# Second network's out stage by one level of Strassen's algorithm, in two passes per group of 768 tokens

## The chip, the cores and the metric

One core of a Trainium2 chip runs the whole program. The metric is the time of one execution on the device in microseconds (us); the median of three executions is quoted. TensorE does the matrix products (PE in the rows; PEld is its loading of weights), VectorE (DVE), ScalarE (ACT) and GpSimd (POOL) do the elementwise work, SyncE (SP) issues the transfers between the chip's DRAM, where all arrays lie, and the on-chip buffers.

## The reference, cut to what matters

```python
x = attention(q, k, v, f)            # 2304 tokens x 512, causal, with decay; unchanged here
h = x @ w_in                         # 512 x 2048, first network
x = (h / (1 + exp(-h))) @ w_out      # 2048 x 512, "first out stage"
a = x @ w_a                          # 512 x 1536, second network
b = x @ w_b
return (a * b) @ w_out2              # 1536 x 512, "second out stage"
```

Everything is computed from float32 to float32. Each float32 product is done as three matrix products of rounded halves: an operand is split into a high part and the rest (low part), and high times high, high times low and low times high are added up in PSUM.

## The kernel before

**Stages.** After the attention (to about 190 us) come four stages, each of which keeps TensorE full: the first network's in stage, its out stage, the second network's in stage, its out stage. Tokens are handled in 3 groups of 768 (`GT`, two halves of 384 = `HB`).

**In stages.** They already use one level of Strassen's algorithm. The input of a group is cut into 2 x 2 blocks, seven sums of blocks (`FORMS`) are formed and split by `make_forms` into the buffers `X0`, `X1`, `X2`, the weights of a unit by `load_unit` into `wA`, `wB`, `wC`. A `job` (one unit, one group) does seven products (`product`, L709) of 6 matmuls of 128 x 384 and combines them on ACT and DVE (L751 to L792). In the second network it also multiplies a by b and sends the result to the array `cdram` by `send` (L740).

**Out stages.** `out_blocks` takes blocks of 512 tokens (four of them, and one of 256): for each of the 16 (first) or 12 (second) pieces of 128 rows it loads the piece from DRAM into one of seven slots (`ring`, L819), splits it (ACT cast L823, DVE subtraction L824, tile `hl`, tag `u` of three slots) and does 12 matmuls (L832) into four PSUM banks. At a block's end ACT and DVE copy the banks and SP sends them out (L858 to L860). There is no Strassen step here.

**Weights.** They arrive as float64 bits and are decoded by `decode`, piece by piece (128 x 512): a transfer of 512 KB (`raw`, L656), one ACT operation (L658), four DVE operations (L659, L660, L662, L663) and one POOL addition (L664). `load_out` decodes the 12 pieces of the second out stage around its start, and splits them with ACT (L612) and POOL (L613) into the tiles `wo`, which lie in `X2` and `X0` once the in stage's inputs there are used up.

**What sets the order.** All operations are put into a `Plan`, with a duration, a priority and what they read and write; `Plan.order` sorts them by a list schedule, in which every engine takes the operation that can start first. The engines then run the result in that fixed order, each waiting where its next instruction's data or buffer isn't ready. `split` does a cast on ACT and a subtraction on the engine given (`pool` or `ss`, that is POOL or DVE).

Of the kernel before, what the change touches and what calls it, by code (L numbers as in the profile page):

```python
# [18 lines left out]
P = 128  # L19
# [212 lines left out]
def model_kernel(ctx: ExitStack, tc: tile.TileContext, qk, q0, v, f, w, out):  # L232
# [21 lines left out]
    rows_sb = dp.tile([NH, 6, 2, S], BF16, name="rows")  # L254
    gdram = dram.tile([F1, P, NT], F32, name="gdram")
    cdram = dram.tile([F2, P, NT], F32, name="cdram")
# [458 lines left out]
    def bank(tag, name):  # L715
        return buf(mm if tag == "mm" else aps, tag, [P, 512], F32, name)

    def job(stage, u, g, t, early):
# [54 lines left out]
        if stage == 0:  # L773
            gate(1, 1, d, at(4) - 2)
        else:
            z = zbuf()
            dve(HB, lambda e: e.tensor_mul(z()[:, 1], pc(1), pd()), [(c, 1), d], [(z, 0, 1)], at(4) - 2)
# [11 lines left out]
        if stage == 0:  # L789
            gate(1, 0, a, at(6) - 2)  # L790
        else:
            dve(HB, lambda e: e.tensor_mul(z()[:, 0], pc(0), pa()), [a, (c, 0)], [(z, 0, 0)], at(6) - 2)  # L792
            send(0, rows(cdram, u), at(6))

    def load_out(stage, h, slot, pr):
        nf = (F1, F2)[stage] // 2
# [6 lines left out]
        yield  # L803

# [49 lines left out]
    def evict_end(t0, n, ps, p):  # L854
        for oc in range(KC):
            o = buf(zp, "z", [P, n], F32, f"out_{t0}_{oc}")
            reads, writes = [ps[oc]], [o]
            plan.add("ACT", 190 + n / 1.2, lambda o=o, oc=oc: nc.scalar.copy(o(), ps[oc]()[:, :n]), reads, writes, p,  # L858
                     also=[("DVE", 160 + n / 0.96, lambda o=o, oc=oc: nc.vector.tensor_copy(o(), ps[oc]()[:, :n]))])
            plan.dma(480, 4 * P * n, lambda o=o, oc=oc: nc.sync.dma_start(out[oc * P:(oc + 1) * P, t0:t0 + n], o()), [o], [("out", t0, oc)], p)  # L860
# [95 lines left out]
    for n, blocks in enumerate(SETS):  # L956
# [75 lines left out]
```

## Time and profile before

| | |
|---|---|
| median of 3 runs | 969.08 us (968.35 to 969.65) |
| profiled execution | 969.41 us, span 967.5 us |
| granted TensorE clock | 1.0 of full speed |
| first out stage | 353.6 to about 551 us |
| second in stage | about 551 to 816.1 us |
| second out stage | 816.1 to 964.1 us, then 3.4 us to the end |

The span is the time from the first instruction to the last; what the execution has beyond it, 1.9 us, lies around the program. Operations of an engine that is not waited for cost nothing, so each number below counts only where TensorE would wait for it, or at the end of the program.

### The profile page before, as it was taken

To read this page: it belongs to the slowest core of one execution; us is meant where nothing else is said; L and a number is where in the kernel's file an instruction comes from. 1 tells how busy PE (TensorE), PEld (TensorE's weight loads), DVE (VectorE), ACT (ScalarE), POOL (GpSimd) and SP (SyncE) were. 2 spreads that over 40 slices of the span, in tenths; PEclk is the share of its full clock that TensorE was granted. 3 is DMA by queue.
4 is the path that set the end of the run, shared out by engine and by line. 5 is a ranking of instruction groups with operands and counts; after the bars stand their busy time and mean duration, and the time that the engine had idled before them with its cause. 6 is when DMAs were issued, how large, how long until landed. Compare 5 with 4: busy or idle time off the path is not lost.

```text
span 967.5 us, 16086 instructions
## 1 busy us (share of the span) xinstructions
PE 959.0 (99%) x5760; PEld 854.4 (88%) x5760; DVE 649.0 (67%) x1284; ACT 483.6 (50%) x1067; POOL 383.7 (40%) x350
## 2 busy tenths in 40 slices
PE   8999999999999999999999999999999999999998
PEld 7766666899999998888888999999999999888888
DVE  7878898985777889778622685765655684932222
ACT  5898888955566664347332543433333332423222
POOL 5677886102585435455100034754444450510000
PEclk9999999999999999999999999999999999999999
DMA  5544433222455586354431103423233336446422
GB/s 154 178 164 146 152 118 114 86 107 106 159 202 185 171 304 221 103 181 142 142 98 49 39 34 110 137 93 109 93 116 109 115 93 228 163 112 184 134 67 93
DMA packets 56560, 128.41 MB, mean 133 GB/s; under 512 B 9500, under 2 KB 14764, under 8 KB 56448
## 3 DMA queue, kind: packets, MB, share of 16 engines
q1 hardware_dynamic: 56368, 126.94, 40.2%
q8 instruction: 45, 0.74, 0.3%
q10 hardware_dynamic: 112, 0.45, 0.2%
q14 instruction: 35, 0.29, 0.1%
HBM read 89.08 MB, written 38.26 MB: 132 GB/s over the span
## 4 chain that ended last, share of the span: by engine, by line
PE 90%; DVE 5%; DMA 1%; ACT 1%; issue 1%; SPq 1%; POOL 0%; DVEq 0%; ACTq 0%
PE o L832 34%; PE a L709 25%; PE b L709 12%; PE g L709 6%; PE s L450 4%; PE pv L572 3%; PE t_x L526 2%; PE t_y L526 2%; DMA rb<-invs 1%; DVE x L613 1%; DVE z L626 1%; DVE p L476 1%; PE idle L297 1%; PE s L444 1%; SPq L505 1%
## 5 line engine op out<-in xcount | busy, mean ns | idle before, releaser
L832 PE MATMUL o<-hl,wo 128*128 128x512 f32 (+1 forms) x1680 | 346.4, 368 | 0.1
L832 PEld LDWEIGHTS o<-hl,wo 128*128 128x128 f32 x1680 | 292.6, 189 | 53.5 <-DVE hl L824 1.3
L709 PE MATMUL a<-x,w 128*128 128x384 f32 x1440 | 270.4, 334 | 0.1
L709 PEld LDWEIGHTS a<-x,w 128*128 128x128 f32 x1440 | 251.2, 188 | 0.8 <-DVE d L772 0.5
L824 DVE TENSOR_TENSOR hl<-ring,hl 128x512 fp32r<-128x512 f32 (+1 forms) x140 | 104.1, 746 | 144.7 <-ACT hl L823 141.5
L613 POOL TENSOR_TENSOR w<-e,w 128x512 fp32r<-128x512 f32 x80 | 96.1, 1213 | 212.0 <-ACT w L612 211.5
L664 POOL TENSOR_TENSOR e<-m,e 128x512 f32<-128x512 f32 x68 | 97.8, 1443 | 188.3 <-DVE e L663 164.4
L823 ACT CAST hl<-ring 128x512 fp32r<-128x512 f32 (+1 forms) x140 | 80.9, 580 | 175.2 <-PE o L832 165.0
L709 PE MATMUL b<-x,w 128*128 128x384 f32 x720 | 143.9, 334 | 0.0
L709 PEld LDWEIGHTS b<-x,w 128*128 128x128 f32 x720 | 126.3, 188 | 0.0
L484 ACT ACTIVATE p<-p,nm 128x512 f32<-128x512 f32 (+3 forms) x128 | 70.7, 561 | 5.4 <-DVE nm L476 5.1
L709 PE MATMUL g<-x,w 128*128 128x384 f32 x360 | 72.1, 334 | 0.0
L709 PEld LDWEIGHTS g<-x,w 128*128 128x128 f32 x360 | 63.3, 188 | 0.1
L751 ACT COPY c<-a 128x384 f32<-128x384 f32 x60 | 28.8, 479 | 67.3 <-PE a L709 51.7
L402 POOL TENSOR_TENSOR qkl<-qk,qkh 128x304 fp32r<-128x304 f32 x60 | 53.4, 918 | 19.3 <-DVE qkh L394 18.8
L476 DVE CUSTOM_DVE_ANT_0 p<-s,maskw 128x512 f32<-128x512 f32 (+3 forms) x128 | 56.4, 483 | 6.3 <-PE t_y L526 1.7
L772 DVE TENSOR_TENSOR d<-a,c 128x384 f32<-128x384 f32 x60 | 33.8, 564 | 39.4 <-PE a L709 39.0
L660 DVE SCALAR_TENSOR_TENSOR m<-raw,m 128x512 uint32<-128x512 uint32 x68 | 59.0, 869 | 1.0
L663 DVE SCALAR_TENSOR_TENSOR e<-raw,e 128x512 f32<-128x512 uint32 x68 | 57.6, 855 | 0.3
L612 ACT CAST w<-e 128x512 fp32r<-128x512 f32 x80 | 44.2, 567 | 26.7 <-POOL e L684 11.7
L756 ACT COPY c<-b 128x384 f32<-128x384 f32 x60 | 28.8, 480 | 52.7 <-PE b L709 52.7
L759 ACT COPY c<-a 128x384 f32<-128x384 f32 x60 | 28.8, 479 | 50.3 <-PE a L709 50.1
(115 smaller groups left out, 1199.4 us busy)
## 6 DMA issues: line engine op xcount, KB each, us to landing
raw<-in_w SPq DMA_DIRECT2D x68, 512.0 KB
gdram<-z SPq DMA_DIRECT2D x44, 384.0 KB
ring<-gdram SPq DMA_DIRECT2D x64, 256.0 KB
cdram<-z SPq DMA_DIRECT2D x36, 384.0 KB
ring<-cdram SPq DMA_DIRECT2D x48, 256.0 KB
qk<-in_qk SPq DMA_DIRECT2D x15, 608.0 KB
vt<-in_v SPq DMA_DIRECT2D x16, 320.0 KB
rb<-invs SPq DMA_DIRECT2D x32, 128.0 KB
```

Of the source, the lines that this page charges most:

```text
L402: plan.add("POOL", t_pool(QK // 4), lambda c=c: nc.gpsimd.tensor_sub(lo()[:, c], raw()[:, c], hi().bitcast(F32)[:, c]), [(hi, "h"), raw], ...
L476: plan.add("DVE", t_dve(nj) + 82, lambda out=out, low=low, o=o, mk=mk: nc.vector.tensor_tensor_reduce(out(), o(), mk, -SCALE, 3.0e38, ALU. ...
L484: plan.add("ACT", t_act(sum(IB[ib]), 279), lambda b=b, c=c, nj=sum(IB[ib]): nc.scalar.activation(b()[:, :nj], b()[:, :nj], AF.Exp, bias=nm ...
L612: act(n, lambda: nc.scalar.copy(hi(), val()), reads, [key + (0,)], pr)
L613: eng(n, lambda e: e.tensor_sub(lo(), val(), hi().bitcast(F32)), list(reads) + [key + (0,)], [key + (1,)], pr)
L660: plan.add("DVE", 690, lambda: nc.vector.scalar_tensor_tensor(u(m), high(), 0x80000000, u(m), ALU.bitwise_and, ALU.bitwise_or), [raw], [m] ...
L663: plan.add("DVE", 690, lambda: nc.vector.scalar_tensor_tensor(e(), low(), 2.0 ** -52, e(), ALU.mult, ALU.mult), [raw], ek, pr, port=True)
L664: pool(n, lambda g: g.tensor_add(e(), m(), e()), [m], ek, pr)
L709: nc.tensor.matmul(ps()[:, :HB], a, b, start=start and k == 0 and i == 0, stop=k == 1 and i == 2, skip_group_check=not start)
L823: act(n, lambda hl=hl, g=g: nc.scalar.copy(hl()[:, 0], g()), [(ring, i)], [(hl, 0)], p - 6)
L824: ss(n, lambda e, hl=hl, g=g: e.tensor_sub(hl()[:, 1], g(), hl()[:, 0].bitcast(F32)), [(hl, 0), (ring, i)], [(hl, 1)], p - 6)
L832: nc.tensor.matmul(ps[oc]()[:, :n], a, m, start=f == 0 and i == 0, stop=f == nf - 1 and i == 2)
```

## The change

The second out stage is rewritten (`out_pairs` in place of `out_blocks`). Its 1536 rows are taken as 6 pairs of 256, its 512 columns as two halves, a group's tokens as two halves of 384. For each group two passes go over the 6 pairs: the first does the four products 2, 3, 4, 5 of the seven, the second 6, 7, 1. A product is 6 matmuls of 128 x 384, three into each of two PSUM banks. Between the passes and at a group's end ACT keeps copies of four results and DVE combines them into `parts`, from which SP sends them out.

- `send_sums`: the in stage now writes three arrays of 384 per unit and group (both halves and their sum, one more addition on DVE or POOL) instead of two, in one transfer of 576 KB instead of 384 KB.
- `decode_out`: the 12 weight pieces are decoded in the first out stage (after its first two blocks) and written to DRAM (`wdram`).
- `load_pairs`: they are read back two pieces at a time; 5 additions and 4 splits make the 7 forms of each pair (tiles `wo`), on POOL or DVE, whichever the plan finds free (`either`).
- `pair`: two transfers of 384 KB per pair and pass (tiles `c`), one DVE operation that forms a difference or a sum (`d`), two casts on ACT and two subtractions on DVE into one of four slots (`few` in `wB`, three in `more` in `X1`).

```diff
-    cdram = dram.tile([F2, P, NT], F32, name="cdram")
+    cdram = dram.tile([F2, P, NG, 3, HB], F32, name="cdram")
...
+        def send_sums(p):
+            either(HB, lambda e: e.tensor_add(z()[:, 1], z()[:, 0], z()[:, 2]), [(z, 0, 0), (z, 0, 1)], [(z, "s")], p)
+            plan.dma(480, 12 * P * HB, lambda: nc.sync.dma_start(cdram[u, :, g], z()), [(z, 0, 0), (z, 0, 1), (z, "s")], [("c", u, g)], p + 1)
...
+    def decode_out(n, pr):
+        e = decode(piece_of(1, "out") + n, (), pr)
+        plan.dma(480, 4 * P * PIECE, lambda: nc.sync.dma_start(wdram[n], e()), [(e, 0), (e, 1)], [("w", n)], pr)
...
+    def load_pairs(h, slot, pr):
...
+            form(0, 2, 0, 3)
+            combine(1, 1, 3, True)
+            combine(2, 2, 0, True)
+            form(2, 2, 1)
+            combine(0, 0, 3, True)
+            combine(1, 1, 0, False)
+            form(4, 1, 0)
+            combine(2, 0, 2, False)
+            form(5, 2, 1)
...
+            if second:
+                ss(HB, lambda e: e.tensor_add(tmp()[:, 0], raw()[:, 0], raw()[:, 3]), rk, [tmp], p - 6)
+                sets = ((2, 2, lambda: raw()[:, 1:3], rk), (1, 1, lambda: tmp()[:, :1], [tmp]))
+            else:
+                ss(2 * HB, lambda e: e.tensor_sub(flat(tmp()[:, :2]), flat(raw()[:, :2]), flat(raw()[:, 2:])), rk, [tmp], p - 6)
+                sets = ((0, 2, lambda: raw()[:, ::3], rk), (2, 2, lambda: tmp()[:, :2], [tmp]))
...
+        for g in range(NG):
...
+            for v in range(2 * PAIRS):
+                t = pair(g, v, False, ps, (3, 4, 5, 2) if v == last else (2, 3, 4, 5), t)
...
+            keep(0, 3, p - 3)
+            keep(1, 4, p - 3)
+            for o in range(2):
+                mix(0, 5, o, 0, True, p - 2)
+                send_out(0, 0, 1, o, p)
...
+            for v in range(2 * PAIRS):
+                t = pair(g, v, True, ps, (1, 6, 7) if v == last else (6, 7, 1), t)
...
+        if n:
+            for i in range(F2 // 3):
+                decode_out((n - 1) * F2 // 3 + i, 1000 + t - 24 + 6 * i)
...
-    hooks[11, 1] = [lambda p=1000 + end(0) - 10: [g.send(()) for g in (begun(load_out(1, 0, 2, p)),) for _ in range(F2 // 2)]]
-    late_half = lambda p=1000 + end(F2 // 2) - 14: begun(load_out(1, 1, 0, p + 16))
+    hooks[11, 0] = [lambda p=1000 + end(0): load_pairs(0, 2, p - 12)]
+    hooks[11, 1] = [lambda p=1000 + end(0): load_pairs(1, 0, p - 2)]
```

The order of the instructions is the same up to the first out stage's third block. Three places differ where the prediction speaks of them.

The first is DVE in the first out stage, in its fourth block (tokens 1536 to 2047). Rows `hl` are the subtractions that the next matmuls need; `m` and `e` belong to the decoding of a piece. Before:

```order
L824 TENSOR_TENSOR hl0_1536_3_5940<-ring0_4762,hl0_1536_3_5940 128x512
L824 TENSOR_TENSOR hl0_1536_4_5957<-ring0_4762,hl0_1536_4_5957 128x512
L824 TENSOR_TENSOR hl0_1536_5_5973<-ring0_4762,hl0_1536_5_5973 128x512
L824 TENSOR_TENSOR hl0_1536_6_5989<-ring0_4762,hl0_1536_6_5989 128x512
L824 TENSOR_TENSOR hl0_1536_7_6005<-ring0_4762,hl0_1536_7_6005 128x512
```

After, at the same place:

```order
L870 TENSOR_TENSOR hl0_1536_3_5996<-ring0_4763,hl0_1536_3_5996 128x512
L669 SCALAR_TENSOR_TENSOR e_63_5994<-raw_63_5921,e_63_5994 128x512
L665 TENSOR_SCALAR m_64_6001<-m_64_6001 128x512
L870 TENSOR_TENSOR hl0_1536_4_6016<-ring0_4763,hl0_1536_4_6016 128x512
L666 SCALAR_TENSOR_TENSOR m_64_6001<-raw_64_5974,m_64_6001 128x512
L668 TENSOR_SCALAR e_64_6040<-m_64_6001 128x512
L870 TENSOR_TENSOR hl0_1536_5_6038<-ring0_4763,hl0_1536_5_6038 128x512
L669 SCALAR_TENSOR_TENSOR e_64_6040<-raw_64_5974,e_64_6040 128x512
L665 TENSOR_SCALAR m_65_6045<-m_65_6045 128x512
L870 TENSOR_TENSOR hl0_1536_6_6062<-ring0_4763,hl0_1536_6_6062 128x512
```

Between two `hl` rows there are now two to four operations of the decoding.

The second is POOL from the last jobs of the second in stage on (`z1` is the sum of a job, `wo` a weight form's low part, L839 an addition of weight blocks). Before, each piece took an addition (`e`) and a subtraction (`wo`):

```order
L664 TENSOR_TENSOR e_61_8696<-m_61_8645,e_61_8696 128x512
L613 TENSOR_TENSOR wo_1_0_8529<-e_61_8696,wo_1_0_8529 128x512
L664 TENSOR_TENSOR e_62_8967<-m_62_8944,e_62_8967 128x512
L613 TENSOR_TENSOR wo_1_1_8994<-e_62_8967,wo_1_1_8994 128x512
L664 TENSOR_TENSOR e_63_8990<-m_63_8950,e_63_8990 128x512
```

After, the last rows of POOL in the program:

```order
L839 TENSOR_TENSOR m_4_8853<-m_4_8853 128x256 x2
L753 TENSOR_TENSOR z1_9_2_8938<-z1_9_2_8938 128x384
L619 TENSOR_TENSOR wo_1_1_8885<-m_4_8853,wo_1_1_8885 128x512
L839 TENSOR_TENSOR m_5_8966<-m_5_8966 128x256
L619 TENSOR_TENSOR wo_1_1_8885<-m_5_8966,wo_1_1_8885 128x512
L839 TENSOR_TENSOR m_5_8966<-m_5_8966 128x256 x2
L753 TENSOR_TENSOR z1_10_2_9024<-z1_10_2_9024 128x384
L619 TENSOR_TENSOR wo_1_1_8885<-m_5_8966,wo_1_1_8885 128x256
L619 TENSOR_TENSOR wo_1_1_8885<-m_5_8966,wo_1_1_8885 128x512
```

From the point at which `X2` is free, POOL has 9 subtractions of 128x512, 4 of 128x256, 16 additions of 128x256 and 3 sums of 128x384; DVE has 9, 2 and 10 of the first three. The decodings have left this place.

The third is the end of DVE's program, after the last matmuls (`m1`, `m3`, `m4` are products in PSUM, `parts` what is sent out). Before, it ends with one copy for the last block, beside three on ACT:

```order
L824 TENSOR_TENSOR hl1_2048_8_9914<-ring1_8798,hl1_2048_8_9914 128x256
L824 TENSOR_TENSOR hl1_2048_9_9929<-ring1_8798,hl1_2048_9_9929 128x256
L824 TENSOR_TENSOR hl1_2048_10_9944<-ring1_8798,hl1_2048_10_9944 128x256
L824 TENSOR_TENSOR hl1_2048_11_9959<-ring1_8798,hl1_2048_11_9959 128x256
L859 COPY out_2048_2_9988<-o1_2048_2_9801 128x256
```

After:

```order
L978 TENSOR_TENSOR parts_9325<-m1_2_0_10151,saved_9301 128x384 x2
L978 TENSOR_TENSOR parts_9325<-m1_2_1_10155,saved_9301 128x384 x2
L1005 TENSOR_TENSOR parts_9325<-parts_9325,m3_2_0_9946 128x384
L1005 TENSOR_TENSOR parts_9325<-parts_9325,m4_2_0_9956 128x384
L1005 TENSOR_TENSOR parts_9325<-parts_9325,m4_2_1_9960 128x384
L1005 TENSOR_TENSOR parts_9325<-parts_9325,m3_2_1_9950 128x384
```

Eight operations of DVE now follow the last `m1` product. TensorE's program ends with the two halves of `m3` and then of `m4`, 12 matmuls.

## Rows read from the trace of the kernel before

**Rows 1.** The page: busy time, share of the span, instructions of an engine.

```profile
PE 959.0 (99%) x5760; PEld 854.4 (88%) x5760; DVE 649.0 (67%) x1284; ACT 483.6 (50%) x1067; POOL 383.7 (40%) x350
...
PEclk9999999999999999999999999999999999999999
```

**Rows 2.** The chain that ended last: start us, us, what, matmuls.

```profile
353.57 2.76 PE o L832 x12
...
815.03 1.06 PE a L709 x6
816.10 147.99 PE o L832 x720
```

**Rows 3.** Busy time by stretch: us, each engine (instructions), clock, DMA share, GB/s.

```profile
610.00:810.00 200.00, 200.00 (x1155) 200.00 (x1155) 126.55 (x219) 71.55 (x140) 95.71 (x90) 1.00 0.33 110
...
440.00:485.00 45.00, 45.00 (x200) 37.28 (x199) 31.05 (x41) 23.24 (x42) 12.30 (x10) 1.00 0.46 134
485.00:530.00 45.00, 45.00 (x200) 37.25 (x199) 12.08 (x18) 11.51 (x20) 0.00 (x0) 1.00 0.26 72
...
772.40:816.10 43.70, 43.70 (x253) 43.67 (x253) 29.23 (x48) 14.64 (x28) 13.53 (x10) 1.00 0.40 132
...
816.10:852.00 35.90, 35.90 (x159) 29.52 (x159) 30.26 (x37) 14.27 (x25) 16.79 (x12) 1.00 0.59 188
852.00:941.00 89.00, 89.00 (x395) 73.68 (x394) 25.32 (x36) 25.67 (x44) 1.19 (x1) 1.00 0.42 125
...
816.10:964.10 148.00, 147.98 (x720) 125.10 (x719) 62.32 (x88) 46.53 (x84) 17.98 (x12) 1.00 0.43 133
```

**Rows 4.** Timeline of ACT in the last block of 256: start us, us, operation.

```profile
951.16 0.41 ACT L823 CAST hl<-ring 128x256 fp32r<-128x256 f32 x1 [1.03 <-PE o L832]
952.60 0.41 ACT L823 CAST hl<-ring 128x256 fp32r<-128x256 f32 x1 [1.03 <-PE o L832]
```

**Rows 5.** Groups by line: shapes and count | busy us, mean ns | idle before.

```profile
L709 PEld LDWEIGHTS a<-x,w 128*128 128x128 f32 x1440 | 251.2, 188 | 0.8 <-DVE d L772 0.5 <-issue 0.2
...
L660 DVE SCALAR_TENSOR_TENSOR m<-raw,m 128x512 uint32<-128x512 uint32 x68 | 59.0, 869 | 1.0
L663 DVE SCALAR_TENSOR_TENSOR e<-raw,e 128x512 f32<-128x512 uint32 x68 | 57.6, 855 | 0.3
...
L662 DVE TENSOR_SCALAR e<-m 128x512 uint32<-128x512 uint32 x68 | 43.5, 648 | 1.5 <-POOL wo L613 0.4
L659 DVE TENSOR_SCALAR m<-m 128x512 uint32<-128x512 uint32 x68 | 41.4, 611 | 7.1 <-ACT m L658 5.9 <-ACT z L731 1.2
...
L664 POOL TENSOR_TENSOR e<-m,e 128x512 f32<-128x512 f32 x68 | 97.8, 1443 | 188.3 <-DVE e L663 164.4 <-PE o L832 14.8 <-DMA ring<-gdram 9.1
...
L824 DVE TENSOR_TENSOR hl<-ring,hl 128x512 fp32r<-128x512 f32 (+1 forms) x140 | 104.1, 746 | 144.7 <-ACT hl L823 141.5 <-DMA ring<-cdram 3.0 <-DMA ring<-gdram 0.2
...
L613 POOL TENSOR_TENSOR wo<-e,wo 128x512 fp32r<-128x512 f32 x28 | 39.5, 1414 | 28.0 <-ACT wo L612 21.1 <-issue 6.9
...
L684 POOL TENSOR_TENSOR e<-e 128x256 f32<-128x256 f32 x40 | 33.4, 836 | 2.0
...
L613 DVE TENSOR_TENSOR x<-z,x 128x768 fp32r<-128x768 f32 x35 | 35.4, 1038 | 1.5 <-ACT x L612 1.5
...
L786 DVE TENSOR_TENSOR c<-g,c 128x384 f32<-128x384 f32 x36 | 20.0, 555 | 13.5 <-PE g L709 11.9
```

**Rows 6.** Timeline of DVE and POOL, first out stage.

```profile
371.34 1.78 DVE L824 TENSOR_TENSOR hl<-ring,hl 128x512 fp32r<-128x512 f32 x1
...
374.10 0.68 DVE L824 TENSOR_TENSOR hl<-ring,hl 128x512 fp32r<-128x512 f32 x1
...
371.14 1.43 POOL L613 TENSOR_TENSOR wo<-e,wo 128x512 fp32r<-128x512 f32 x1 [0.73 <-ACT wo L612]
```

**Rows 7.** Busy time in one microsecond at full DMA load.

```profile
809.00:810.00 1.00, 1.00 (x7) 1.00 (x6) 0.68 (x2) 0.31 (x1) 0.00 (x0) 1.00 1.02 381
```

**Rows 8.** The chain that ended last, its last piece.

```profile
964.11 0.37 ACT out L858
```

More of the change, by code (lines that the diff above doesn't have):

```diff
@@ L34 @@
 SCALE = 1.0 / math.sqrt(D)
+PAIRS = FF2 // (4 * P)
 U1, U2 = FF1 // (2 * P), FF2 // P
@@ L254, in model_kernel @@
     rows_sb = dp.tile([NH, 6, 2, S], BF16, name="rows")
+    wdram = dram.tile([F2, P, PIECE], F32, name="wdram")
     gdram = dram.tile([F1, P, NT], F32, name="gdram")
-    cdram = dram.tile([F2, P, NT], F32, name="cdram")
+    cdram = dram.tile([F2, P, NG, 3, HB], F32, name="cdram")
     pools = {"wA": wp, "wB": wp}
@@ L605, in pool, with either @@
         plan.add("POOL", 240 + 2.2 * n, lambda: fn(nc.gpsimd), reads, writes, prio)
+    def either(n, fn, reads, writes, prio):
+        plan.add("POOL", 240 + 2.2 * n, lambda: fn(nc.gpsimd), reads, writes, prio,
+                 also=[("DVE", 100 + n / 0.88, lambda: fn(nc.vector))], port=True)
     def ss(n, fn, reads, writes, prio):
@@ L776, in job @@
             z = zbuf()
-            dve(HB, lambda e: e.tensor_mul(z()[:, 1], pc(1), pd()), [(c, 1), d], [(z, 0, 1)], at(4) - 2)
+            if g == NG - 1 and u in (U2 - 3, U2 - 2):
+                first.append(inner(0, len(first), False))
+            dve(HB, lambda e: e.tensor_mul(z()[:, 2], pc(1), pd()), [(c, 1), d], [(z, 0, 1)], at(4) - 2)
         yield at(5)
@@ L792, in job @@
             dve(HB, lambda e: e.tensor_mul(z()[:, 0], pc(0), pa()), [a, (c, 0)], [(z, 0, 0)], at(6) - 2)
-            send(0, rows(cdram, u), at(6))
+            send_sums(at(6))
     def load_out(stage, h, slot, pr):
-        nf = (F1, F2)[stage] // 2
+        nf = F1 // 2
         t = wouts[stage, h] = buf(None, f"X{slot}", [P, nf, 2, DM], F32R, f"wo_{stage}_{h}")
@@ L803, in load_out, with form, combine @@
         yield
+    def decode_out(n, pr):
+        e = decode(piece_of(1, "out") + n, (), pr)
+        plan.dma(480, 4 * P * PIECE, lambda: nc.sync.dma_start(wdram[n], e()), [(e, 0), (e, 1)], [("w", n)], pr)
+    def load_pairs(h, slot, pr):
+        t = wouts[1, h] = buf(None, f"X{slot}", [P, PAIRS, 2, FORMS, 2 * P], F32R, f"wo_1_{h}")
+        for k in range(PAIRS):
+            p, v = pr + 4 * k * T_PROD / 1000, PAIRS * h + k
+            m = buf(dcp, "raw", [P, 4, 2 * P], F32, f"m_{v}")
+            keys = [(m, q) for q in range(4)]
+            plan.dma(480, 8 * P * PIECE, lambda m=m, v=v: nc.sync.dma_start(
+                m().rearrange("p (f i) c -> p f (i c)", f=2), wdram[2 * v:2 * v + 2].rearrange("f p c -> p f c")),
+                [("w", 2 * v), ("w", 2 * v + 1)], keys, p - 4)
+            def form(f, n, q, step=1, m=m, keys=keys, k=k):
+                end = q + (n - 1) * step + 1
+                hi, lo = (lambda i=i: t()[:, k, i, f:f + n] for i in range(2))
+                split(n * 2 * P, hi, lo, lambda: m()[:, q:end:step], keys[q:end:step], (t, k, f), p, either)
+            def combine(o, a, b, add, m=m, keys=keys):
+                either(2 * P, lambda e: (e.tensor_add if add else e.tensor_sub)(m()[:, o], m()[:, a], m()[:, b]), [keys[a], keys[b]], [keys[o]], p)
+            form(0, 2, 0, 3)
[7 more added lines that the diff above has]
+            form(5, 2, 1)
     AHEAD, marks = 1, {}
@@ L852, in evict_mid @@
             a = e
[L854 to L860, printed above, removed]
+    W2, W5, W1, W6, W7 = 2, 3, 4, 5, 6
@@ L967, in model_kernel @@
     hooks[0, 0] = [U(1, 2, place(2, 0) - 30)]
-    hooks[11, 1] = [lambda p=1000 + end(0) - 10: [g.send(()) for g in (begun(load_out(1, 0, 2, p)),) for _ in range(F2 // 2)]]
-    late_half = lambda p=1000 + end(F2 // 2) - 14: begun(load_out(1, 1, 0, p + 16))
+    hooks[11, 0] = [lambda p=1000 + end(0): load_pairs(0, 2, p - 12)]
+    hooks[11, 1] = [lambda p=1000 + end(0): load_pairs(1, 0, p - 2)]
     t = stage_in(1, U2, seq, hooks, t)
-    ring = buf(None, "wA", [P, 7, 512], F32, "ring1")
-    for n, blocks in enumerate(SETS):
-        t = out_blocks(1, blocks, ring, t, evict_end, None if n else late_half())
+    t = out_pairs(t)
     order = keep_warm(plan.order())
```

86 lines of the change are left out of this document (83 added, 3 removed).

## Prediction

> **What bounds the kernel now.** I read the page's busy times first: TensorE 99% at a granted clock of 9 tenths or more in every slice [rows 1]. A busy share alone could be filled up by waits, so the chain that ended last comes next: from 816.10 on it is one piece of 147.99 us, the 720 matmuls of the second out stage, without a gap, and the in stage before it runs in steps of 1.04 us per product of 6 [rows 2]. The stretches say the same: TensorE is busy for the whole of each [rows 3]. So any matmul time taken away here comes off the end, as long as nothing else becomes late; every other engine has room on average, and the question is where it has none.
>
> **The products.** Three widths can be read. In the 512-wide out blocks 12 matmuls take 2.76 us in a piece that stands alone [rows 2]; the 384-wide in stage does 1155 in 200.00 us [rows 3], that is 173.2 ns each, or 1.04 per 6. In the last block of 256 the cast that waits for TensorE comes every 1.44 us, once per 12 matmuls, so 120 ns each [rows 4]. Removed are 576 matmuls of 512 and 144 of 256, the 147.99 us. Added are 3 groups x 6 pairs x 7 products x 6 = 756 of 384 columns, the shape of the in stage: 126 products x 1.04 = 131.04 us. The term is **-16.95 us**, less than an eighth since there are 36 matmuls more.
>
> Would the loading of weights stop this? One load is busy for 188 ns [rows 5], longer than the 173.2 or the 120 ns in which a matmul of 384 or 256 is done with a fresh load each. So the loads overlap and set no floor at this width. The Trainium skill (TensorE: Matmul & The Clock Gate, Back-to-back issue gap) says that the spacing in a stream of loads and matmuls is set by both, which speaks against adding loads; if the loads alone set it, the gain would be 5.9 us (rival 3) instead of 16.95. The trace of the 256-wide block does not bear that reading out.
>
> **The decoding that moves.** Twelve pieces leave the stretch around 816 and go into the first out stage, behind its second block, that is between about 440 and 530. Each brings four DVE operations, 0.869 + 0.855 + 0.648 + 0.611 = 2.98 us, one POOL addition of 1.44 [rows 5], a 512 KB read and a 256 KB write. In those 90 us DVE is now busy 31.05 + 12.08 = 43.1 us and POOL 12.3 [rows 3]; with 35.8 and 17.3 more it is 78.9 and 29.6. It fits, but only if it lies evenly: on DVE the decoding stands in front of the `hl` subtractions, and TensorE waits for those. A step of 12 matmuls is 2.7 us (395 in 89.00 us [rows 3]); with three `hl` slots a subtraction may end two steps after its slot is free before TensorE feels it, so some 4 us of other work fit in front of it beside its cast and itself. Going down the new order of DVE with these means, with 0.75 per `hl`, 1.04 per operation of 768 and 2.7 us per step, the backlog rises to some 2.5 us in the fourth block and falls again. DVE is in the same state now from 816.10 to 852.00, 30.26 of 35.9 us with POOL at 16.79, and TensorE loses nothing there [rows 3]. The writes to `wdram` wait for POOL in SP's queue, with the ring's loads behind them; the ring holds seven loads, up to 19 us. I take **+0.3 us**; bounds 0 (as that stretch) and 3 (the backlog once over the slack).
>
> **In stage.** 36 sums are added, 26 on DVE, 10 on POOL, at most 0.75 us each on DVE (the 512-wide row), under 20 us in 265; DVE is busy 126.55 of 200 there, DMA at a share of 0.33 [rows 3], and the transfers grow by half. Nothing of it is waited for by TensorE but through the four `z` slots, one job (7.28 us) apiece. 0, and 0 to 1 if a slot comes late.
>
> **Hand-over.** This is the place I trust least. The forms of pairs 0 to 2 go into `X2`, free 6 jobs before the end (about 772.4), those of pairs 3 to 5 into `X0`, free 3 jobs before it; the last are needed 3 x 4 products into the new stage, 12.5 us after 816.1. POOL has 9 subtractions of 1.41, 20 operations of 256 at 0.84 [rows 5] and 3 sums between 0.84 and 1.41: about 33 us. DVE has 9 + 12 of the same work (at most 0.75 each, 15.7 us), 24 combinations of the last six jobs at 0.555, 13.3 us, and sums, differences and first splits, 6.4 us: about 35 us. Together 68 us in 56.2, 1.21 per us. Now DVE and POOL together do 30.26 + 16.79 = 47 us in 35.9, 1.31 per us, and TensorE is busy for all of it [rows 3]. What is more, 12 decodings of 2.98 on DVE have left. Behind POOL stand two things that others wait for: SP holds the `c` loads of pairs 1 and 2 behind the sums of the last jobs, and the first pair's split on DVE (`few`) stands behind the weight forms.
>
> Against that stand pairs of rows on how the two engines meet: an `hl` subtraction that starts 0.20 us into a POOL operation of 1.43 takes 1.78 us, one with POOL idle 0.68 [rows 6]. It waits for POOL's operation to end. If each of DVE's operations here had to wait its turn so, the in-order combinations too, all 68 us would run one after the other and end 11.8 us late. The row of 816 to 852, where such meetings are as dense and cost TensorE nothing, is nearer. I take **+1.0**, bounds 0 and 12. The Trainium skill (SBUF — State Buffer, Who interferes with whom) states the port that DVE and GpSimd share as an exclusive lock, kept for a whole instruction; by that sentence alone the hand-over would cost the 11.8. The trace agrees with the lock (1.78 against 0.68), not with the loss.
>
> **Inside the new stage.** Operands: pass 1 takes 3 operations of 768 per pair on DVE, 1.038 each [rows 5], 3.1 us for 4.16 of TensorE; pass 2 one such and two of 384, at most 0.75, 2.5 for 3.12. With 36 combinations at 0.555 DVE has at most 122 us in 131, the pairs three slots ahead of TensorE. ACT has about half of that. Transfers: 18 pairs x 2 passes x 768 KB and 4.7 MB of output, 33.0 MB in 131 us, 252 GB/s where the stage moves 133 now; one microsecond at full load moved 381 at a share of 1.02 [rows 3, 7]. So about 0.7 of what DMA can do: it holds. Group boundaries: the next group starts with products 2, 5, 2, whose banks are free, 3.1 us before it needs a bank that DVE is still emptying. 0, bounds 0 and 3.
>
> **End.** Now TensorE ends at 964.09 and ACT's copy of 0.37 follows [rows 8], then the transfers to 967.5. After, the last `m1` half ends 12 matmuls, 2.08 us, before TensorE; four combinations start with its first half, 2.5 before, and end about 0.3 before; four more at 0.555, one of them bound to the very last matmul, end about 1.9 after it, where the copy now ends 0.4 after. **+1.4 us**, bounds 0.9 and 2.
>
> **Sum.** 969.41 (the profiled execution) - 16.95 + 0.3 + 1.0 + 1.4 = 955.2. The median lies 0.33 below that execution, so 954.8.
>
> **The rivals.** (1) *The hand-over starves TensorE*: price 4 to 12 us more, 959 to 966, for the reasons above. For it speaks the 1.78; against it that the work moved away is larger than the work put there. (2) *The transfers become the bound* and the kernel is slower. Each input is now read in both passes; if the queue delivers under 33.0 MB / 146 us = 226 GB/s, the gain is gone. At the 188 GB/s that 816 to 852 shows it would take 176 us, 28 more than now: about 999. For it: 188 is the most that any stretch of 30 us listed here moved. Against: its share was 0.59, so that DMA was asked for no more, and 381 is there at full share. (3) *The load of weights is the floor* at this width: 756 loads of 188 ns one after the other, 142.1 us, 5.9 less than now, so 966. Against it stand the 120 ns of [rows 4]. (4) *Stalls eat the gain to within the error*: hand-over and first out stage both at their upper ends, 967 to 971. The change does what it says: the order shows 756 new matmuls and no old ones.
>
> **How the numbers follow.** The likeliest, a stage that stays full with small stalls: 0.74, 952.5 to 958. Rival 1: 0.13. Rival 3: 0.02. Rival 4: 0.04. Rival 2 and a first out stage that stalls for more than 15 us: 0.07. A measurement of this kernel can tell about 0.2%, 1.9 us, from no change. Faster: 0.74 + 0.13 + 0.02, less 0.01 of rival 1's far end, 0.88; the same 0.05; slower 0.07. The range from 952.4 (no stall, the shorter end) to 962 holds the likeliest and about half of rival 1, 0.81.
>
> **What would show it.** Right: the second out stage's matmuls 131 us from first to last with the in stage's last product at about 816; the chain of waits all TensorE there; DVE at 0.8 to 0.9 of it; decodings between 440 and 530 with TensorE full. Wrong: TensorE idle at 812 to 835 before a `few` or `more` row that waits for DVE, or a `wo` row that waits for POOL (rival 1); ACT or DVE waiting on `c` transfers with a DMA share at 1 (rival 2); 188 ns per matmul (rival 3). The in stage's end after 818 would say that the decoding cost more where it went than I allow.

## The result, and the profile after

The changed kernel takes 955.74 us (median of 4; 954.46 to 956.36) against 968.72 before: ratio 0.9863, 95% interval 0.9846 to 0.988. The profiled execution took 955.71 us with a span of 953.9. So it is faster by 13 us, 1.3%. But at the hand-over from the in stage to the last stage TensorE loses four times what the sum allowed there.

The page's busy times, which answer to [rows 1]:

```profile
PE 942.7 (99%) x5796; PEld 861.1 (90%) x5796; DVE 740.4 (78%) x1412; ACT 511.6 (54%) x1100; POOL 419.8 (44%) x379
```

The share of TensorE is 99% as before, with 36 matmuls more, as counted. DVE has gained 91 us of work, ACT 28, POOL 36.

The loads of weights for the new products, as one group of instructions:

```profile
L921 PEld LDWEIGHTS m<-more,wo 128*128 128x128 f32 x558 | 96.9, 188 | 0.2 <-DVE more L619 0.2
```

The chain that ended last, its pieces at the hand-over and behind it (start us, us, what, instructions); they answer to [rows 2]:

```profile
811.15 1.08 POOL m L839
...
812.25 0.43 DVE m L839
...
814.02 1.75 DVE few L619
815.77 0.04 issue
815.82 3.25 PE m L921 x11
819.07 1.53 PE a L715 x6
820.60 126.52 PE m L921 x729
```

From 820.60 on TensorE works without a gap, 173.3 ns per matmul, as the 384-wide in stage did. Ahead of it stands what was not there before: a split of `few` on DVE, and then 17 matmuls that take 4.78 us where 17 x 173.3 ns are 2.95. Followed further back, the chain lies on POOL from 796.7 to 812.2, with gaps of 0.5 us at most: additions (`m`) and low parts (`wo`) of weight forms, and one sum `z`.

Waits of TensorE from 545 us to the end: us in total, times, longest. It is the only row:

```profile
PE m L921 <- DVE few L619: 2.0, 1, 2.0
```

Timeline of TensorE there (start us, us, operation, idle before):

```profile
813.48 0.34 PE L921 MATMUL m<-few,wo 128*128 128x384 f32 x1
815.82 3.25 PE L921 MATMUL m<-few,wo 128*128 128x384 f32 x11 [2.00 <-DVE few L619]
818.86 1.74 PE L715 MATMUL a<-x,w 128*128 128x384 f32 x6
```

The timelines of ACT, DVE and POOL in the same microseconds:

```profile
811.49 0.83 ACT L618 CAST few<-d_False 128x768 fp32r<-128x768 f32 x1
...
812.25 0.43 DVE L839 TENSOR_TENSOR m<-m 128x256 f32<-128x256 f32 x1 [0.17 <-POOL m L839]
812.60 1.50 DVE L619 TENSOR_TENSOR few<-c_False,few 128x768 fp32r<-128x768 f32 x1
814.02 1.74 DVE L619 TENSOR_TENSOR few<-d_False,few 128x768 fp32r<-128x768 f32 x1
...
811.15 2.13 POOL L839 TENSOR_TENSOR m<-m 128x256 f32<-128x256 f32 x2
813.25 1.70 POOL L753 TENSOR_TENSOR z<-z 128x384 f32<-128x384 f32 x1
814.91 2.68 POOL L619 TENSOR_TENSOR wo<-m,wo 128x256 fp32r<-128x256 f32 x2
```

The first pair's casts were done on ACT at 812.3. DVE stood until 812.25 behind a combination of the sixth pair's weights (`m`) that waits for POOL, and those weights are needed some 27 us later. Then both splits ran beside POOL and took 1.50 and 1.74 us instead of the 0.95 that the second pair's took at 821.70 and 822.57, with POOL idle. The first product that is issued is product 3, whose second matmul reads the split of the difference `d`, the second of the two. It came at 815.76, and would have been due at 813.65, one matmul behind the first. Of these 2.1 us, by an estimate from the rows, 1.3 are the lengthening of the two splits (3.24 less twice 0.95) and some 0.5 the combination ahead of them with its wait for POOL.

Busy time by stretch (us, each engine, granted clock, DMA share, GB/s), which answers to [rows 3]:

```profile
610.00:810.00 200.00, 200.00 (x1155) 200.00 (x1155) 141.78 (x238) 73.31 (x147) 115.70 (x109) 1.00 0.38 135
440.00:485.00 45.00, 45.00 (x201) 37.26 (x200) 42.58 (x55) 25.12 (x45) 18.37 (x14) 1.00 0.65 207
485.00:530.00 45.00, 45.00 (x202) 37.37 (x201) 32.35 (x51) 16.94 (x30) 11.27 (x8) 1.00 0.66 202
772.40:816.10 43.70, 41.70 (x241) 41.38 (x240) 36.94 (x55) 21.16 (x42) 35.41 (x31) 1.00 0.46 155
816.10:852.00 35.90, 35.90 (x199) 35.73 (x199) 30.63 (x44) 19.33 (x30) 1.49 (x2) 0.95 0.95 327
852.00:941.00 89.00, 89.00 (x515) 89.00 (x514) 66.93 (x96) 43.01 (x64) 0.00 (x0) 1.00 0.68 226
813.48:949.71 136.23, 134.23 (x763) 133.42 (x762) 102.75 (x147) 62.79 (x95) 4.11 (x3) 0.99 0.70 235
...
817.00:818.00 1.00, 1.00 (x5) 1.00 (x4) 1.00 (x1) 0.00 (x0) 0.59 (x1) 0.50 0.86 166
819.00:820.00 1.00, 1.00 (x5) 1.00 (x4) 0.34 (x1) 0.00 (x0) 0.00 (x0) 0.50 1.13 379
```

Two things are to be seen. First, the last stage, from its first product to TensorE's end (813.48 to 949.71), takes 136.23 us. It holds 756 matmuls of its own and 6 of the in stage; at 173.3 ns these are 132.1, so 4.1 us are lost, all before 820.60: 2.17 of wait (813.65 to 815.82), 1.83 of slower matmuls, and the rest is the time by which a last matmul outlasts its 173 ns. Second, the slower matmuls have the granted clock at 0.50, the lower of the two levels, from some 817 to 820, and TensorE had waited 2.0 us just before.

The span of this execution is 13.6 us shorter. That is 16.95 for the products, less 4.1 at the hand-over, less 0.8 at the end (TensorE's end to the span's end: 949.71 to 953.9, 4.2 us, where [rows 8] leave 3.4), and 1.6 that came ahead of the stage: six matmuls of the in stage, 1.04 us, stand behind the first product, so that stage would have ended at 814.5, against 816.1 in [rows 2]. This last is scatter, as far as can be told: the same kernel profiled once more (experiment 5) begins the last stage at 815.03, which gives 816.1, and experiments 1 to 11 begin it between 812.64 and 815.59. There is only one profile of the kernel before to hold against them. So the length of the last stage, in the trace, tells more than a time does, and each experiment below is given with both.

### The profile page after: what moved, and what is told of

Same layout as the page of the kernel before. It is cut to its first block, busy times and chain, and to the rows that moved or that the text cites. A ratio compares the mean times of both kernels' runs of the same rounds, so it can differ in the third digit from the quotient of the medians.

```text
span 953.9 us, 16429 instructions
## 1 busy us (share of the span) xinstructions
PE 942.7 (99%) x5796; PEld 861.1 (90%) x5796; DVE 740.4 (78%) x1412; ACT 511.6 (54%) x1100; POOL 419.8 (44%) x379
## 4 chain that ended last, share of the span: by engine, by line
PE 90%; DVE 4%; POOL 2%; DMA 1%; issue 1%; SPq 1%; ACT 1%; DVEq 0%; POOLq 0%
PE a L715 25%; PE o L878 21%; PE m L921 14%; PE b L715 12%; PE g L715 6%; PE s L452 4%; PE pv L574 3%; PE t_x L528 2%; PE t_y L528 2%; DMA rb<-invs 1%; POOL m L839 1%; POOL wo L619 1%; DVE p L478 1%; PE idle L299 1%; PE s L446 1%
## 5 line engine op out<-in xcount | busy, mean ns | idle before, releaser
L878 PE MATMUL o<-hl,wo 128*128 128x512 f32 (+1 forms) x960 | 197.9, 368 | 0.0
L878 PEld LDWEIGHTS o<-hl,wo 128*128 128x128 f32 x960 | 167.4, 189 | 30.2 <-DVE hl L870 0.4
L619 POOL TENSOR_TENSOR w<-e,w 128x512 fp32r<-128x512 f32 x80 | 100.9, 1272 | 151.7 <-ACT w L618 151.5
L921 PE MATMUL m<-more,wo 128*128 128x384 f32 x558 | 98.8, 334 | 0.0
L921 PEld LDWEIGHTS m<-more,wo 128*128 128x128 f32 x558 | 96.9, 188 | 0.2 <-DVE more L619 0.2
L870 DVE TENSOR_TENSOR hl<-ring,hl 128x512 fp32r<-128x512 f32 (+1 forms) x80 | 67.4, 845 | 30.5 <-ACT hl L869 29.8
L869 ACT CAST hl<-ring 128x512 fp32r<-128x512 f32 (+1 forms) x80 | 46.3, 580 | 75.2 <-PE o L878 63.7
L761 ACT COPY c<-a 128x384 f32<-128x384 f32 x60 | 28.7, 479 | 60.6 <-PE a L715 44.5
```

The lines of the kernel that those rows point to most:

```text
L619: eng(n, lambda e: e.tensor_sub(lo(), val(), hi().bitcast(F32)), list(reads) + [key + (0,)], [key + (1,)], pr)
L869: act(n, lambda hl=hl, g=g: nc.scalar.copy(hl()[:, 0], g()), [(ring, i)], [(hl, 0)], p - 6)
L870: ss(n, lambda e, hl=hl, g=g: e.tensor_sub(hl()[:, 1], g(), hl()[:, 0].bitcast(F32)), [(hl, 0), (ring, i)], [(hl, 1)], p - 6)
L878: nc.tensor.matmul(ps[oc]()[:, :n], a, m, start=f == 0 and i == 0, stop=f == nf - 1 and i == 2)
L921: nc.tensor.matmul(ps[o]()[:, :HB], a, b, start=start and i == 0, stop=stop and i == 2, skip_group_check=not fresh)
```

## Experiments

They are told in the order in which they ran. "Stage" is the time from the first product of the last stage to TensorE's end, 136.2 us in the changed kernel. Where the granted clock stays at 1.00, the same kernel's would be some 134.4 (136.2 less 1.83, an estimate); an experiment whose clock did not fall is to be held against that as well. "Mean clock" is the granted clock over the whole of one execution.

**1. The two splits of the first pair swapped.**

```
-  ... reads, key + (c,), p - 5, ss)
+  ... reads, key + (c,), p - 5 - 3 * c * ((g, v, second) == (0, 0, False)), ss)
```

> Edit: of the first pair's two splits the one of the differences (d) goes ahead of the one of the loaded inner values (c) on ScalarE and VectorE; every other instruction stays. Theory (the 4.0 us at the hand-over come from one late split: the first product issued is product 3, whose second matmul reads the split of d, which stands second): the wait of TensorE shrinks from 2.0 us by one split (1.5 to 1.7 us), to 0.3 to 0.6 us, and the fall of the granted clock behind it is less or gone: 955.7 less 1.6 to 3.4, so 952.3 to 954.1. Rival A (the sum of VectorE's work at the hand-over decides, whatever the order): 955.7, as the wait moves to the second product. Rival B (the clock falls because the stage changes, whatever the wait): 954.0, with the granted clock at 0.5 for some 4 us all the same.

954.56 us (953.9 to 956.13), ratio 0.986 (0.9845 to 0.9874); stage 135.2. The waits of TensorE at the hand-over:

```profile
PE m L921 <- DVE c L798: 1.3, 1, 1.3
PE m L921 <- DVE few L619: 0.7, 2, 0.3
```

The wait for `few` shrank as the theory had it, but 1.3 us appeared for a bank that DVE empties (L798), behind the same two splits and a difference of 1.80 us. The waits together are no shorter, 2.0 us. The clock stayed at 1.00, which is all that was gained: against 134.4 the stage is no shorter. Late is not one split but whatever comes last on DVE.

**2. The sixth pair's weight forms placed behind the first splits.**

```
+  held = plan.dma(...)
...
+  if v in (5,):      # the sixth pair
+      late_loads.append(held)
...
+  if (g, v, second) == (0, 0, False):      # the first pair's splits
+      for op in late_loads:
+          op.deps.add(plan.ops[-1])
```

> Edit: the weight forms of the sixth pair of pieces (m_5), which are needed some 20 us into the stage, are placed behind the first pair's splits; nothing is left out. Theory (order and the port shared with GpSimd make the splits late): VectorE's first split starts at once when its cast is there, about 811.7 instead of 812.6, and runs beside less GpSimd work; TensorE's wait shrinks from 2.0 us to 0.5 to 1.2 us, the clock's fall costs less too: 952.5 to 954.5. Rival A (VectorE's amount of work decides): part of the forms leaves the window as well, so it gives the same 953 to 954.5; this run alone does not tell A apart, the next one does. Rival C (the splits wait for their casts on ScalarE and not for VectorE's turn): 955.5, wait still 2 us.

955.53 us (954.73 to 957.1), ratio 0.9869 (0.9854 to 0.9884); stage 135.1. The load of the sixth pair's pieces, and with it their forms, now follows the first pair's splits. With POOL idle these took 0.95 us each and the first pair's four products had no wait; then

```profile
PE m L924 <- DVE more L619: 1.0, 2, 0.6
```

by 830 us, for the second pair's splits (1.50 and 2.03 us), which the moved forms on POOL now lengthened, and 0.4 more for the fourth pair's at 832. The wait moved on again; against 134.4 the stage is no shorter.

**3. All weight forms on DVE.**

```
-  split(n * 2 * P, hi, lo, ..., (t, k, f), p, either)
+  split(n * 2 * P, hi, lo, ..., (t, k, f), p, ss)
-  either(2 * P, lambda e: ... m()[:, o], m()[:, a], m()[:, b]) ...
+  ss(2 * P, lambda e: ... m()[:, o], m()[:, a], m()[:, b]) ...
```

> Edit: all weight forms of the last stage on VectorE, none on GpSimd (27 instructions move, some 13 us of VectorE at 0.42 to 0.68 us each), and m_5's last forms fall behind the first splits. Theory (GpSimd beside VectorE lengthens the two splits from 0.95 to 1.5 and 1.75 us, and VectorE waits for GpSimd's forms): both splits take 0.95 us, TensorE's wait is 0 to 0.7 us, 952 to 954. Rival A (VectorE's amount of work decides): 790 to 813.5 us has 19.7 us of VectorE work now and gets 8.3 more less about 3.7 of lock, 24.3 of 23.5 us, so the splits come 1 to 3 us later than now: wait 3 to 5 us, 957 to 960.

953.73 us (952.82 to 954.47), ratio 0.9848 (0.9834 to 0.9863); stage 134.0. More instructions on DVE, and TensorE waits less, 0.5 and 0.7 us:

```profile
PE m L921 <- DVE more L619: 0.7, 1, 0.7
PE m L921 <- DVE few L619: 0.5, 1, 0.5
```

So it is not the count of DVE's instructions, as rival A had it: from 790 to 813 DVE was busy for 21.71 us with 43 of them, against 19.20 with 30 in the changed kernel. Two things came together, though: some of the sixth pair's forms fell behind the first splits, as expected; and of the 2.2 us less, 1.8 are the clock, which did not fall. What POOL does beside DVE is paid for by DVE: a split took 0.94 us beside an idle POOL and 1.78 when POOL's sum of `z` (811.63, 1.35 us) ran:

```profile
812.01 1.78 DVE L619 TENSOR_TENSOR few<-c_False,few 128x768 fp32r<-128x768 f32 x1
813.71 0.94 DVE L619 TENSOR_TENSOR few<-d_False,few 128x768 fp32r<-128x768 f32 x1
```

The remaining 0.7 is for the second pair's splits. They are written to `more`, which lies in `X1`, where the last product of the in stage still reads, 2.1 us before they are due; whether that is enough by itself the sixth experiment shows.

**4. Twelve more matmuls behind the wait.**

```
+  for _ in range(fill):      # 12 ahead of the first pair's product 2, elsewhere 0
+      nc.tensor.matmul(ps[0]()[:, :HB], wt()[:, k, 0, f, :P], x()[:, 0, fx], start=True, stop=True)
```

> Edit: 12 extra matmuls of 128x384 into the bank of product 2 (their sum is thrown away by that product's start) stand ahead of product 2 of the first pair; nothing else changes. Product 2 is the third product issued, so 12 x 0.173 = 2.08 us are added behind the wait and not in it. Theory as far as the clock goes: the fall of the granted clock is caused by the 2.0 us without a matmul, which stays, so the extra matmuls cost 2.1 us at full clock: 957.8; if the clock is still at half when they run, up to 4.2 us, 959.9, and the products behind them then run at full clock: between 957.8 and 958.5. Rival (TensorE has slack in this stage, and the transfers or VectorE set its pace): 955.7, as the extra matmuls vanish in later waits.

957.17 us (956.91 to 958.59), ratio 0.9889 (0.9873 to 0.9906); stage 137.2, or 135.1 without the added 2.08. The three executions with a mean clock of 1.000 have a median of 956.97, 2.5 us above those of the changed kernel in which the clock did not fall (954.46, experiment 5): the 2.08, and a second wait of 0.35 us for a bank that DVE empties. The added work is paid in full, so TensorE has no slack here and the rival falls. What was not expected: the wait was there and the clock did not fall.

```profile
816.00 2.20 PE L923 MATMUL m<-few,wo 128*128 128x384 f32 x11 [1.98 <-DVE few L619]
818.04 1.21 PE L715 MATMUL a<-x,w 128*128 128x384 f32 x6
```

Eleven matmuls in 2.20 us, where the changed kernel took 3.25, and they stand ahead of the added ones.

**5. The changed kernel again.**

> The changed kernel itself once more, unedited, beside the three that follow. It had a granted clock of 0.5 for some 3.8 us behind its 2.0-us wait; the first four experiments had waits of up to 2.0 us and no such fall. Theory (the fall follows the wait in some executions and not in others): time 954.5 to 956.4, and the profiled execution either shows the fall, then its span from the first product to the last is 136.2 us, or does not, then 134.4 us. Rival (the fall is tied to this order of instructions): the fall at the same place again.

956.1 us (953.95 to 957.27), ratio 0.9869 (0.9852 to 0.9886); stage 136.2, with the wait of 2.00 us at 817.37 and the fall behind it. Busy time by stretch there:

```profile
818.00:819.00 1.00, 1.00 (x5) 1.00 (x5) 1.00 (x2) 0.00 (x0) 1.00 (x1) 0.50 1.08 304
```

In the profiled execution the fall came at the same place again, which both the theory and the rival allow. But of the four executions two have a mean clock of 0.998 (957.27 and 956.27 us), two of 1.000 (955.93 and 953.95). So the fall follows in some executions. Of the changed kernel's eight, the five with 0.998 have a median of 956.27 us and the other three of 954.46: 1.8 us apart, as much as the slower matmuls cost in the trace.

**6. The weight forms of pairs 4 to 6 left out.**

```
-  hooks[11, 1] = [lambda p=1000 + end(0): load_pairs(1, 0, p - 2)]
+  hooks[11, 1] = [lambda: wouts.__setitem__((1, 1), wouts[1, 0])]
```

> Leaves out the weight forms of pairs 4 to 6: their products take the forms of pairs 1 to 3, so the output is of other weights; all matmuls, splits, loads of inner values and evictions stay. It takes 15 combinations and 12 splits away from VectorE and GpSimd between 797 and 818 us. Theory now (VectorE's amount of work in the 20 us around the hand-over, lengthened by GpSimd, is the limit; whichever instruction is put ahead, another is late): the wait before the first products goes, and what stays is at most the 0.7 us for the second pair, whose place in memory is released by the last product of the in stage; 132.3 to 133.2 us from the first product to the last instead of 136.2, 951.7 to 953. Rival (one late split, whatever the load): as the order of the splits is as before, a wait of 1 to 2 us stays and the time is 954 to 955.7.

952.09 us (950.93 to 952.99), ratio 0.9829 (0.9814 to 0.9844); stage 132.4, no wait of TensorE:

```profile
812.64 2.27 PE L921 MATMUL m<-few,wo 128*128 128x384 f32 x12
814.75 1.20 PE L715 MATMUL a<-x,w 128*128 128x384 f32 x6
815.79 2.24 PE L921 MATMUL m<-few,wo 128*128 128x384 f32 x12
817.87 1.34 PE L921 MATMUL m<-more,wo 128*128 128x384 f32 x6
```

The order of the splits is untouched and the wait is gone: the 3.8 us by which the stage is shorter, 2.0 of wait and 1.8 of clock, are the price of these three pairs' forms. Their 12 casts on ACT and their loads are left out as well, so the run alone does not say which engine it was; that it was DVE and POOL is read from the chain and from experiment 3. The second pair's place in `X1` costs nothing by itself either: 2.1 us are enough when DVE has no weight forms beside the splits.

**7. Two pieces decoded instead of twelve.**

```
-  decode_out((n - 1) * F2 // 3 + i, ...)
+  if n == 1 and i < 2: decode_out((n - 1) * F2 // 3 + i, ...)
...
-  wdram[2 * v:2 * v + 2]
+  wdram[0:2]
```

> Leaves out 10 of the 12 decodings in the first out stage (and their 10 writes to memory); the last stage loads the first two decoded pieces six times, so the output is of other weights. Theory (the moved decoding is hidden behind that stage's matmuls): 955.7, within 0.7. Rival (decoding costs the first out stage time, up to the 3 us of the prediction's bound): 953 to 955.

956.45 us (955.07 to 956.81), ratio 0.987 (0.9854 to 0.9887); stage 136.2. Ten decodings less give nothing back: where they were moved to, they are hidden. In the changed kernel's own trace TensorE has no wait between 350 and 550 us.

**8. The hand-over relieved.** Forms on DVE as in 3, the fifth and sixth pair's held as in 2 (behind the splits of pairs 2 and 4), the splits as in 1, and

```
+  spare = buf(None, "wA", [P, 1, 2, 4, HB], F32R, "spare")
-  places = cycle([(few, 0)] + [(more, i) for i in range(3)])
+  places = chain([(few, 0), (spare, 0)], cycle([(more, i) for i in range(3)] + [(few, 0)]))
```

> Edits together, nothing left out: all weight forms of the last stage on VectorE; those of the fifth and sixth pair placed behind the splits of the second and fourth pair; the difference's split of the first pair first; the second pair's splits written where unit 9's weights were, which are free, instead of where the last products of the in stage still read. Theory (VectorE's load at the hand-over, GpSimd beside it, and the release of the second pair's place): no wait over 0.5 us at the hand-over, 132.3 to 133.2 us from the first product to the last, 951.5 to 953. Rival (the waits only move on again, to the fifth or sixth pair's forms): 953.5 to 955.5, with a wait of TensorE for wo between 826 and 840 us.

954.17 us (952.98 to 955.22), ratio 0.9851 (0.9836 to 0.9866); stage 133.5. No wait in the stage before 836, but the rival came true in part, for a split and not for `wo`:

```profile
836.42 2.19 PE L925 MATMUL m<-more,wo 128*128 128x384 f32 x11 [0.72 <-DVE more L619]
```

Two pairs' forms behind the hand-over are too many: on DVE they stood ahead of the fifth pair's split (835.42 to 836.36).

**9. Only the sixth pair's forms held**, behind the third pair's splits; all else as 8.

> As the eighth experiment, but only the sixth pair's weight forms are held, behind the third pair's splits (the fifth pair's stay ahead of the hand-over). Theory: of VectorE's work between 815 and 837 us 4.6 us fewer than there, so the 0.72-us wait for the sixth pair's split goes; 132.3 to 132.9 us from the first product to the last (133.5 there, 136.2 in the changed kernel), 951.5 to 953. Rival (VectorE's load before the hand-over now makes the first splits late again): a wait of 0.5 to 1.5 us for the first pair, 133.2 to 134.5 us.

952.77 us (951.92 to 953.7), ratio 0.9835 (0.9822 to 0.9847); stage 133.1, a little over the range. The 0.72-us wait of 8 is gone; it was for the fifth pair's split, not for the sixth's, as the expectation has it. One wait is left, 0.5 us, for `spare`, that is for the second pair; the rival had it for the first.

**10. As 9, with product 1 of the last pair earlier.**

```
-  (1, 6, 7) if v == last else (6, 7, 1)
+  (1, 6, 7) if v >= last - 1 else (6, 7, 1)
-  ... ps[name], p)
+  ... ps[name], p - 3 * step * (name == 1 and v == last))
```

> As the ninth, and in each second pass product 1 of the last pair stands ahead of products 6 and 7 of the last two pairs. Theory (the end is four sums for products 2 and 5 that follow product 1, four for 6 and 7 behind them, and a transfer): the first four are done before the last product, so the time from TensorE's end to the span's end falls from 4.35 to 3.9 us, 0.4 less than the ninth: by the trace only, since 0.4 us is under what the times can tell. Rival (the end is the transfer's, or VectorE is late with the last pairs' splits as product 1 asks for them earlier): no change, or a new wait of 0.3 to 1 us at 942 to 946.

952.11 us (951.33 to 953.63), ratio 0.9829 (0.9816 to 0.9842); stage 133.1. By the trace the end is shorter, TensorE's end at 947.75, the span's at 951.1, 3.35 us instead of 4.2. Of the eight closing sums of DVE, the first four, then the last four:

```profile
943.10 1.95 DVE L986 TENSOR_TENSOR parts<-m,saved 128x384 f32<-128x384 f32 x4 [6.50 <-PE m L925]
946.22 2.12 DVE L1013 TENSOR_TENSOR parts<-parts,m 128x384 f32<-128x384 f32 x4 [1.17 <-PE m L925]
```

Against the changed kernel's

```profile
947.15 1.95 DVE L978 TENSOR_TENSOR parts<-m,saved 128x384 f32<-128x384 f32 x4 [8.58 <-PE m L921]
949.01 1.94 DVE L1005 TENSOR_TENSOR parts<-parts,m 128x384 f32<-128x384 f32 x4
```

the last four sums start 1.5 us ahead of TensorE's end instead of 0.7. The end is shorter by 0.85 us, more than the 0.4 expected. The times of 9 and 10 can't be told apart; together (9 executions, median 952.42) they lie 3.4 us below the changed kernel's eight (median 955.85).

**11. The pieces decoded at the hand-over**, not in the first out stage.

```
+  m = [decode(piece_of(1, "out") + 2 * v + i, (), p - 4) for i in range(2)]
-  plan.dma(..., wdram[2 * v:2 * v + 2] ...)
-  decode_out((n - 1) * F2 // 3 + i, 1000 + t - 24 + 6 * i)
```

> Undoes one part: the 12 pieces of the last stage's weights are decoded where they are turned into forms, in the 45 us ahead of the hand-over, and not in the first out stage; forms are made one piece at a time. Adds there 12 decodings of four VectorE instructions (some 2.2 us each, 26 us), one of ScalarE and one of GpSimd (1.4 us). Theory (VectorE's and GpSimd's amount of work around the hand-over is the limit): VectorE was busy 38 of 48 us there, so 15 us or more don't fit; TensorE waits 10 to 20 us in all, 965 to 976. Rival (the hand-over's cost is one late split, and the pairs' forms have 4 us each to follow): 957 to 960.

976.37 us (975.72 to 977.73), ratio 1.008 (1.0067 to 1.0093); stage 157.0. Waits of TensorE in that stage:

```profile
PE m L921 <- DVE more L619: 10.1, 4, 5.9
PE m L921 <- DVE few L619: 3.7, 2, 3.0
PE a L715 <- DVE d L782: 2.3, 1, 2.3
PE m L921 <- ACT more L618: 1.4, 1, 1.4
```

17.5 us of waits and a granted clock of 0.72 over 813 to 837; the time is just over the upper edge of what was expected. The same products with the decoding done here make the kernel slower than before.

**12. Half as many transfers more.**

```
+  plan.dma(..., nc.sync.dma_start(gdram[v, :, :GT]..., cdram[2 * v, :, g, ::2]), ...)      # one per pair and pass
```

> Adds a copy of 393 KB inside the chip's memory beside each of the 36 pairs' loads (786 KB), 14 MB in all; nothing is left out. The changed kernel's last stage has a share of 0.71 and 240 GB/s, with 308 GB/s over 830 to 870 us and 383 GB/s at its densest. Theory (transfers have room, TensorE sets the pace): 955 to 957.5, the stage at 136 us plus nothing, and a share of 0.9 or more. Rival (the transfers were close to their limit): half as much again is 360 GB/s over the stage, past the 240 to 308 that hold so far; TensorE waits for loads in the second passes, 960 to 985.

962.09 us (960.79 to 967.09), ratio 0.9942 (0.9921 to 0.9962). Stage 135.2, and the loss lies ahead of it. Busy time by stretch:

```profile
700.00:819.65 119.65, 117.84 (x676) 116.78 (x675) 82.86 (x135) 43.89 (x91) 69.59 (x64) 1.00 0.57 189
819.65:954.82 135.17, 132.82 (x763) 131.86 (x762) 102.21 (x147) 62.28 (x95) 4.11 (x3) 1.00 0.71 242
830.00:850.00 20.00, 20.00 (x118) 20.00 (x117) 15.08 (x21) 11.15 (x19) 0.00 (x0) 1.00 1.01 366
```

Most copies were issued before the stage: there are only 7 GB/s more in it than the changed kernel's 235. So it does not tell what the stage would bear; it shows 366 GB/s at a share of 1.01 over 20 us with TensorE full. The time lies in the rival's range, but its mechanism, waits for loads in the second passes, is not there. Why the in stage lost some 5 us (2.9 of waits for ACT's copies are seen) was not followed up.

## Why the prediction was right, and where it was not

955.74 lies in the range of 952.4 to 962.0 and 0.9 above the forecast of 954.8. Step by step:

- **Products, -16.95: right.** 515 matmuls in 89.00 us, the outer ones cut by the window, are 172.8 ns each. The loads of weights lie beside them, 188 ns apiece (group L921 PEld), so rival 3 is wrong at this width too.
- **Decoding in the first out stage, +0.3: right.** TensorE is busy 45.00 of 45.00 us in both stretches with DVE at 42.58 and 32.35 (78.9 forecast, 74.9 measured) and POOL at 29.6; experiment 7 gives nothing back.
- **In stage, 0: right.** 1155 matmuls in 200.00 us, with DVE 15 us busier.
- **Hand-over, +1.0: mis-sized, 4.0 measured.** The text names the mechanism that the trace shows, the first pair's split behind the weight forms and lengthened by POOL, and then prices it low. Its size was taken from the stretch of 816 to 852, 1.31 us of DVE and POOL per us, as 68 us in 56.2 were only 1.21. But the work did not spread over 56 us: from 772.4 to 816.1 the two had 36.94 + 35.41 us in 43.7, 1.66 per us; and in the whole of the 56.2 us, 772.4 to 828.6, they were busy for 48.10 + 36.90 = 85.0 us, not 68. In both sums the time is counted twice in which one of them waits for the other within an operation, as in the splits of 1.50 and 1.74 us. The forms of the last three pairs can't be written before `X0` is free, and POOL begins on them at 796.7 after 3.6 us without work; and one of the last of them stands ahead of splits that are due first. The row taken for nearest was not dense enough. And the fall of the clock, 1.83 of the 4.0, was in no term. Experiment 6 gives 3.8 us back, experiments 1 and 2 show that reordering alone moves the wait. Rival 1's sign is there, an idle TensorE before a `few` row that waits for DVE; its price began at 4 more than the forecast, and it came to 3 more.
- **Inside the stage, 0: right.** 729 matmuls in one piece. DVE was busy for 0.75 of the stage, not 0.8 to 0.9. DMA moved 235 GB/s where 252 was worked out. Rival 2 is out: it needed a queue under 226 GB/s, or stuck at the 188 of 816 to 852, and in those very microseconds the changed kernel moved 327, with TensorE busy throughout. The share there is 0.95, so not much is left; how much more the stage would bear stays open after experiment 12.
- **End, +1.4: 0.8 measured**, just under its lower bound: eight sums in a row took 0.48 us each, not 0.555, and the very last ended 1.2 us after TensorE, not 1.9.

The hand-over's 3 us too much are partly made good by the end (0.6 less), by the decoding (0.3 less) and, in the profiled execution, by 1.6 us of scatter ahead of the stage. That the total is nearer than its terms is luck. The range, too, is wider below than its own terms: no stall and the shortest end give 969.08 - 16.95 + 0.9 = 953.0, not 952.4. Rival 4, stalls up to 967, did not come.

## What to carry to other kernels

When operands have to be prepared by the very engines that also feed the stage before, add up their work over the time in which their place in memory is free, not over the whole neighbourhood, and look for a row that dense. Moving one late instruction ahead may only show the next, so take work away first (a decoding moved 300 us ahead, forms kept off GpSimd while VectorE is needed). Of a wait of TensorE, look at the granted clock behind it too: here, where it fell, that cost 1.8 us behind a wait of 2.0.

## What the runs showed of the hardware

After a wait of 2.0 us TensorE worked at a granted clock of 0.50 (1.2 instead of 2.4 GHz) for about 3 us, beginning 0.6 to 0.8 us after it resumed, in three of five profiles with such a wait: in the changed kernel's, 5's and 7's, but not in 4's and 12's. In 12 as in 4 the matmuls behind the wait ran at full speed:

```profile
821.97 2.18 PE L921 MATMUL m<-few,wo 128*128 128x384 f32 x11 [1.98 <-DVE few L619]
```

By the mean clock, 0.998 or less, it fell in 9 of the 16 executions of the changed kernel (twice four), 4 and 7; in the 25 of kernels 1, 2, 3, 8, 9 and 10, whose profiles have waits of 1.3 us at most, in none. (The six executions of 12 have 0.994 to 0.999, but other waits, of up to 1.5 us, stand ahead in that kernel.) In kernel 4 the one execution with 0.998 took 958.59 us, the others 956.91 to 957.37. What decides whether it falls was not settled.

A subtraction of 128x768 on DVE took 0.94 to 0.95 us beside an idle POOL and 1.49 to 2.05 beside POOL's additions and subtractions (the changed kernel, experiments 1 to 3).
